# Score pieces of a fused attention and MLP kernel in other groups: three, three and two instead of four times two

## The chip, the cores and the metric

The kernel runs on one core of a Trainium2 chip. The metric is the time of the whole program on the device, in microseconds (us). Engines are named as in the profile: PE is TensorE, DVE is VectorE, ACT is ScalarE, POOL is GpSimd, SP is SyncE; PEld is the loading of weights into PE.

## What is computed

Inputs are q, k, v of 4 batches x 8 heads x 768 tokens x 64, and a matrix of 8 x 8 per batch and head, `sort_net`. In short:

```python
for _ in range(5):                       # P: rows, then columns brought to sum 1
    P = exp(P - max(P)); P /= sum(P, -1); P /= sum(P, -2)
k_sorted = P @ blocks(k)                 # 8 blocks of 96 tokens, mixed
v_sorted = P @ blocks(v)
attn = softmax(q_b @ k_sorted_b.T / 8)   # within each block of 96 tokens
x = attn @ v_sorted_b                    # -> 3072 tokens x 512
h = relu(x @ w_in)                       # 512 -> 2048
out = (s * h * h + b) @ w_out            # 2048 -> 512
```

The attention gives the 3072 x 512 input of an MLP with a hidden width of 2048. Most of the multiplications are in the MLP.

## The kernel before

**Stages.** The tokens are handled in eight tiles of 384 (a batch has two halves, `half` 0 and 1, of four blocks each). For tile `t`, `ffn1(t)` makes the hidden layer in eight steps: step `i` is 8 matmuls (L473) into a PSUM tile `hps`, then a ReLU on ACT (L485) and a square on DVE (L486). `ffn2(t)` makes the output in three rows of 128 tokens; each row is 16 matmuls (L497) into a PSUM tile `ops`, and one DVE instruction (L522) brings the row to SBUF, from which SP stores it.

**Slots.** The attention of a later tile is put between these matmuls. `ffn1` calls what its dictionary `slots` holds for step `i` after step `i`; `ffn2` has twelve slots, one after each four matmuls (slot `4*m + f//4`), the store of row `m` coming ahead of the pieces in slots 3, 7 and 11. Batch 0's second half is laid into the steps of `ffn1(0)`. Batches n = 1, 2, 3 are made by `halves(n)`, whose second dictionary `s1` fills the slots of `ffn2(2n-1)`. The order of the instructions on every engine is that of the calls; no scheduler moves them.

**Pieces.** A piece is one pair of heads (`hp`) of one half.

- `SC(b, half, hp)`, `s_piece`: 8 score matmuls (L380), two by two, each with 64 rows of K and all four blocks of both heads, into one PSUM tile `sc` of the pool `psa`; then one exponential on ACT (L388, for batch 0 L384), which writes the SBUF tile `at`.
- `SB(hp)`, `s_banks`: the same for batch 0 with the eight matmuls (L398) into two half-size PSUM tiles `scb` of the pool `psb`, and two half-size exponentials (L403).
- `P(b, half, hp)`, `p_piece`: 8 matmuls (L422) of `at` with the sorted V into a tile `pv` of `psa`; then on DVE a reciprocal (L427) and a product (L428), which writes the SBUF tile `x`.
- `V(b, i, engine)`, `v_piece`: 32 matmuls (L328) into a tile `tv` of `psa`, copied on by the engine named. `PDB(n)` is six small DVE instructions that build the mixing matrix of batch n (L273 to L282). `TD` and `TP` transpose `x`, by DMA or on PE.

The score matmuls use half of the rows of PE each, the two heads side by side; matmuls of every other large kind use all rows (the P pieces 112 of them). A run of score pieces with no other matmul between them is called a stretch here.

**Buffers.** The pool `psa` has three tiles, shared by `hps`, `sc`, `pv`, `tv` and the tiles of the sorted K; `psb` has two, shared by `ops`, `scb` and the transposes. A new tile takes the place of an old one, and its first matmul waits until the engine that reads the old one is through. PE takes its instructions in order, so all matmuls behind a waiting one wait too.

Of the kernel before, what the change touches and what calls it, by code (L numbers as in the profile page):

```python
# [22 lines left out]
def kernel(  # L23
# [182 lines left out]
    def q_banks(b, half, engs):  # L206
        if b not in QT:
            QT[b] = trp.tile([128, 2, NHP, CQ, 64], BF, tag="qt", name="qt")
        pr = slice(half * 64, (half + 1) * 64)
        for u in range(2):  # L210
            tr = psb.tile([128, 1024], BF, tag="b", name="tqb")
            for a in range(2 * u, 2 * u + 2):
                for c in range(CQ):
                    for e in range(2):
                        o = (a % 2 * CQ + c) * 64
                        nc.tensor.transpose(out=tr[e * 64:(e + 1) * 64, o:o + 64],
                                            in_=QH[b][pr, 2 * a + e, c, :],
                                            identity=ident[pr, pr])
            evac(engs[u], QT[b][:, half, 2 * u:2 * u + 2].rearrange("p a c t -> p (a c t)"),
                 tr[:, 0:2 * TG])  # L220
# [145 lines left out]
    def s_piece(b, half, hp, sc=None):  # L366
        g0 = hp * NB + half * HB
        if sc is None:
            sc = psa.tile([128, 2, 512], FP, tag="a", name="sc")
        byp = len(QT[b].shape) == 5  # L370
        for n in range(HB):
            for e in range(2):
                pr = slice(e * 64, (e + 1) * 64)
                if byp:
                    o = sc[:, e, 0:TG].rearrange("p (c t) -> p c t", c=CQ)[:, :, 16 * n:16 * n + 16]
                    r = QT[b][pr, half, hp, :, 16 * n:16 * n + 16]
                else:
                    o = sc[:, e, n * BLK:(n + 1) * BLK]
                    r = QT[b][pr, half * HB + n, hp, :]
                nc.tensor.matmul(out=o, lhsT=KS[b % 2][pr, g0 + n].rearrange("p z c -> p (z c)"),  # L380
                                 rhs=r, start=True, stop=True)
        at = atp.tile([KR, 2, TG], BF, tag="at", name="at")
        if byp:
            nc.scalar.activation(out=at.rearrange("p e (t c) -> p e t c", c=CQ),  # L384
                                 in_=sc[0:KR, :, 0:TG].rearrange("p e (c t) -> p e t c", c=CQ),
                                 func=AF.Exp, scale=scale)
        else:
            nc.scalar.activation(out=at, in_=sc[0:KR, :, 0:TG], func=AF.Exp, scale=scale)  # L388
        AT[b, half, hp] = at

    def s_banks(b, half, hp):
        g0 = hp * NB + half * HB
        at = atp.tile([KR, 2, TG], BF, tag="at", name="at")
        sc = [psb.tile([128, TG], FP, tag="b", name="scb") for _ in range(2)]
        for n in range(HB):
            for e in range(2):
                pr = slice(e * 64, (e + 1) * 64)
                nc.tensor.matmul(  # L398
                    out=sc[e].rearrange("p (c t) -> p c t", c=CQ)[:, :, 16 * n:16 * n + 16],
                    lhsT=KS[b % 2][pr, g0 + n].rearrange("p z c -> p (z c)"),  # L400
                    rhs=QT[b][pr, half, hp, :, 16 * n:16 * n + 16], start=True, stop=True)
        for e in range(2):
            nc.scalar.activation(out=at[:, e].rearrange("p (t c) -> p t c", c=CQ),  # L403
                                 in_=sc[e][0:KR].rearrange("p (c t) -> p t c", c=CQ),
                                 func=AF.Exp, scale=scale)
        AT[b, half, hp] = at

    def p_piece(b, half, hp, fill=0):
        g0 = hp * NB + half * HB
        atf = AT.pop((b, half, hp)).rearrange("p e t -> p (e t)")  # L410
        if hp == 0:
            X[b, half] = xp.tile([BLK, HB, d_model], BF, tag="x", name="x")
        x = X[b, half]
        pv = psa.tile([128, 2, 512], FP, tag="a", name="pv")
        for i in range(fill):
            nc.tensor.matmul(out=pv[:, i % 2, 272:512], lhsT=zeros[:, 0:128], rhs=zeros[:, 0:240],  # L416
                             start=True, stop=True)
        for e in range(2):
            for n in range(HB):
                c0 = (e * HB + n) * BLK  # L420
                m = 128 if c0 + 128 <= 2 * TG else BLK
                nc.tensor.matmul(out=pv[0:m, e, n * VW:(n + 1) * VW],  # L422
                                 lhsT=atf[:, c0:c0 + m], rhs=VS[b % 2][:, e * NG + g0 + n, :],
                                 start=True, stop=True)
        pvv = pv[0:BLK, :, 0:HB * VW].rearrange("p e (n w) -> p e n w", w=VW)
        rec = rtp.tile([BLK, 2, HB], FP, tag="rec", name="rec")
        nc.vector.reciprocal(out=rec, in_=pvv[:, :, :, D])  # L427
        nc.vector.tensor_tensor(  # L428
            out=x[:, :, hp * 128:(hp + 1) * 128].rearrange("p n (e d) -> p e n d", e=2),
            in0=pvv[:, :, :, 0:D],  # L430
            in1=rec.unsqueeze(3).broadcast_to([BLK, 2, HB, D]), op=ALU.mult)
# [13 lines left out]
    def t_dma(b, half):  # L445
        x = X.pop((b, half))
        xt = xtp.tile([128, HB, NHP, BLK], BF, tag="xt", name="xt")
        nc.sync.dma_start_transpose(out=xt.rearrange("p n a c -> p (n a) c"),
                                    in_=x.rearrange("p n m -> p (n m)"))
        XT[b * 2 + half] = xt  # L450
# [13 lines left out]
    def part(t, i, hpl, fill=0):  # L464
        if (t, i) not in H1:
            H1[t, i] = psa.tile([128, 2, 512], FP, tag="a", name="hps")
        for j in range(fill):
            nc.tensor.matmul(out=H1[t, i][:, j % 2, TG:512], lhsT=zeros[:, 0:128],
                             rhs=zeros[:, 0:128], start=True, stop=True)
        for f in range(2):  # L470
            for hp in hpl:
                fc = (2 * i + f) * 128
                nc.tensor.matmul(out=H1[t, i][:, f, 0:TG], lhsT=wi[:, hp, fc:fc + 128],  # L473
                                 rhs=XT[t][:, :, hp, :],
                                 start=(hp == 0), stop=(hp == NHP - 1))

    def ffn1(t, slots, done={}):

        gt = gtp.tile([128, NF, TG], BF, tag="gt", name="gt")
        GT[t] = gt  # L480
        for i in range(NF // 2):
            part(t, i, range(done.get(i, 0), NHP))
            rt = rtp.tile([128, 2, TG], BF, tag="rt", name="rt")
            h = H1.pop((t, i))[:, :, 0:TG]
            nc.scalar.activation(out=rt, in_=h, func=AF.Relu)  # L485
            nc.vector.tensor_tensor(out=gt[:, 2 * i:2 * i + 2, :], in0=rt, in1=rt, op=ALU.mult)  # L486
            for p in slots.get(i, ()):
                p()
        XT.pop(t)
# [97 lines left out]
    def QF0(): return lambda: q_banks(0, 1, "AD")  # L587
    def SB(i): return lambda: s_banks(0, 1, i)
# [3 lines left out]
    def SC(b, h, i): return lambda: s_piece(b, h, i)  # L592
    def P(b, h, i): return lambda: p_piece(b, h, i)
# [3 lines left out]
    def TD(b, h): return lambda: t_dma(b, h)  # L597
# [5 lines left out]
    def halves(n):  # L603

        if n == 1:
            s0 = {3: [KP(n, 0, "AD"), KP(n, 1, "AD"), KP(n, 2, "AD")],
                  9: [V(n, 0, "D"), V(n, 1, "A"), V(n, 2, "D")]}
        else:
            s0 = {0: [KP(n, 0), KP(n, 1), KP(n, 2)]}
        s1 = {0: [SC(n, 0, 0), SC(n, 0, 1)],  # L610
              3: [P(n, 0, 0), SC(n, 0, 2), SC(n, 0, 3)], 4: [P(n, 0, 1)], 5: [P(n, 0, 2)],
              6: [P(n, 0, 3), TD(n, 0), SC(n, 1, 0), SC(n, 1, 1)], 8: [P(n, 1, 0)],
              9: [P(n, 1, 1), SC(n, 1, 2), SC(n, 1, 3)], 10: [P(n, 1, 2)],
              11: [P(n, 1, 3), TD(n, 1)]}
        if n == 1:
            s1[0] = [V(n, 3, "A")] + s1[0]
        if n + 1 < B:
            s1[1] = [PDB(n + 1)]
        return s0, s1

    ffn1(0, {0: [QF0()], 2: [SB(0)], 3: [P(0, 1, 0), SB(1)], 4: [P(0, 1, 1), SB(2)],
             5: [P(0, 1, 2), SB(3)],
             6: [TP(0, 1, 0, "A"), TP(0, 1, 1, "D"), P(0, 1, 3)], 7: [TP(0, 1, 2, "A")]},
         {0: 3, 1: 3})
    part(1, 0, (0, 1))
# [11 lines left out]
    s0, s1 = halves(1)  # L637
    ffn2(0, s0)
    ffn2(1, s1)
    for b in range(1, B):  # L640
        n = b + 1
        s0, s1, u0, u1 = {}, {}, {}, {}
        if n < B:
            load("k", n, 6, XT[2 * b + 1][:, HB - 1, NHP - 1, 0:1])
            load_q_rows(n)
            s0, s1 = halves(n)
# [38 lines left out]
```

## Time and profile before

| What | Value |
|---|---|
| median of 3 runs | 222.98 us (222.55 to 224.73) |
| the profiled execution, whole time | 222.54 us |
| its span in the profile | 220.4 us |
| PE busy | 213.6 us, 97% |
| DVE busy | 126.0 us, 57% |
| ACT busy | 109.4 us, 50% |
| POOL busy | 70.8 us, 32% |
| score matmuls L380 / L398 | 200 and 56 |
| granted clock of PE | 0.999 |

The span leaves out what lies before the first and behind the last instruction, here 2.1 us. A row of the timeline gives the start of a run of like instructions on an engine, how long it was busy with them, the engine, the line, what is written and read, and how many they were; in brackets stands the idle time of the engine ahead of them and what ended it. Matmuls overlap, so the time that one takes of PE is read from start to start. A few matmul records are missing in the trace, so the counts of a row can be one short.

### The profile page before, as it was taken

Reading aid. Unit: us, or ns where it says so; the run is one execution under the profiler, and the core shown is the slowest. Engines: PE = TensorE matmul, PEld = TensorE weight load, DVE = VectorE, ACT = ScalarE, POOL = GpSimd, SP = SyncE. Lnnn points to the kernel's source line nnn. Section 1 sums busy time; section 2 is a strip of 40 time slices with the busy share of each in tenths; the row PEclk is TensorE's granted clock in tenths of the full one; section 3 lists DMA queues with packets and bytes.
Section 4 is the critical chain, followed back from the end, with each engine's and each line's share of the span. In section 5 each row is a group of like instructions: output and inputs, shape, how many; then the busy total and the mean of one; then the engine's idle time right before and its main releaser. Section 6 shows DMA issues by size and latency. Waiting matters only on the chain.

```text
span 220.4 us, 5172 instructions
## 1 busy us (share of the span) xinstructions
PE 213.6 (97%) x2156; PEld 128.8 (58%) x2175; DVE 126.0 (57%) x257; ACT 109.4 (50%) x149; POOL 70.8 (32%) x127
## 2 busy tenths in 40 slices
PE   7989999999999999999999999999999999999994
PEld 5877766555465555666446555665446566654454
DVE  6777457567875768547636677547417744441222
ACT  4677687658635445664622535665424356550000
POOL 7659781689832004920050008800000000000000
PEclk9999999999999999999999999999999999999999
DMA  6999999999979662999979846999911940001212
GB/s 154 284 164 125 120 170 204 204 172 134 128 215 181 49 187 41 178 208 121 141 204 175 107 135 88 208 179 102 215 72 48 123 119 3 0 0 48 93 53 95
DMA packets 67255, 28.92 MB, mean 131 GB/s; under 512 B 51872, under 2 KB 63264, under 8 KB 67232
## 3 DMA queue, kind: packets, MB, share of 16 engines
q0 software_dynamic: 31168, 12.85, 49.5%
q1 hardware_dynamic: 36064, 15.74, 35.6%
q8 instruction: 17, 0.28, 0.6%
q14 instruction: 6, 0.05, 0.1%
HBM read 28.85 MB, written 7.86 MB: 167 GB/s over the span
## 4 chain that ended last, share of the span: by engine, by line
PE 90%; DMA 5%; DVE 1%; issue 1%; POOL 1%; ACT 0%; POOLq 0%
PE hps L473 38%; PE ops L497 36%; DMA rawk<-in_k_dram 5%; PE pv L422 4%; PE sc L380 3%; PE tpp L302 2%; PE ops L514 2%; PE tv L328 2%; PE tvr L347 1%; DVE vs L204 1%; PE tr L439 1%; PE scb L398 1%; POOL rawk L93 0%; PE sc L257 0%; PE pv L416 0%
## 5 line engine op out<-in xcount | busy, mean ns | idle before, releaser
L473 PE MATMUL hps<-xt,wi 128*128 128x384 bf16 x512 | 87.9, 326 | 0.0
L497 PE MATMUL ops<-wo,gt 128*128 128x512 bf16 x350 | 82.4, 379 | 1.4 <-issue 0.6
L485 ACT ACTIVATE rt<-hps 128x768 bf16<-128x768 f32 x64 | 51.8, 811 | 39.5 <-PE hps L473 38.3
L473 PEld LDWEIGHTS <-wi 128*128 128x128 bf16 x512 | 49.0, 98 | 32.6 <-issue 0.4
L486 DVE TENSOR_TENSOR gt<-rt 128x768 bf16<-128x768 bf16 x64 | 36.0, 565 | 41.2 <-ACT rt L485 41.0
L497 PEld LDWEIGHTS <-gt 128*128 128x128 bf16 x368 | 34.1, 98 | 37.4
L522 DVE SCALAR_TENSOR_TENSOR ot<-ops,s_bc,bias 128x512 f32<-128x512 f32 (+2 forms) x27 | 18.6, 691 | 34.7 <-PE ops L497 31.6
L388 ACT ACTIVATE at<-sc 112x768 bf16<-112x768 f32 x24 | 18.1, 808 | 30.1 <-PE sc L380 30.1
L428 DVE TENSOR_TENSOR x<-pv,rec 96x512 bf16<-96x512 f32 x32 | 22.0, 686 | 1.1
L115 POOL DMA_DIRECT2D qtok<-in_q_dram x24 | 18.6, 808 | 0.7 <-issue 0.7
L422 PEld LDWEIGHTS <-at 112*128 112x128 bf16 (+1 forms) x256 | 12.9, 101 | 6.7 <-ACT at L388 1.0
L202 ACT CAST ks<-tpp 64x512 bf16<-64x512 f32 x18 | 13.2, 731 | 4.7 <-DVE ks L204 4.1
L140 POOL DMA_DIRECT2D wi<-in_moe_w_in_dram x24 | 12.8, 558 | 5.5 <-DMA rawk<-in_k_dram 3.2
L422 PE MATMUL pv<-vs,at 112*128 112x66 bf16 (+1 forms) x256 | 13.9, 195 | 0.1
L204 DVE CAST ks<-tpp 64x512 bf16<-64x512 f32 x18 | 13.1, 729 | 0.9 <-ACT ks L202 0.5
L93 POOL DMA_DIRECT2D rawk<-in_k_dram x21 | 11.2, 550 | 2.7 <-issue 1.9
L93 POOL DMA_DIRECT2D rawv<-in_v_dram x18 | 9.7, 558 | 6.0 <-DMA wo<-in_moe_w_out_dram 4.6
L130 PE MATMUL z<-zeros 128*64 128x96 bf16 (+2 forms) x129 | 9.8, 241 | 1.3 <-DVE zeros L118 1.2
L90 POOL COPY rawk<-xt 128x1 bf16<-128x1 bf16 x2 | 0.4, 190 | 32.8 <-DMA xt<-x 32.8
L427 DVE RECIPROCAL rec<-pv 96x8 f32<-96x8 f32 x32 | 6.4, 200 | 6.4 <-PE pv L422 6.4
L130 PEld LDWEIGHTS <-zeros 128*64 128x64 bf16 (+1 forms) x130 | 7.5, 115 | 3.0 <-DVE zeros L118 1.2
L349 DVE CAST rawv<-tvr 128x512 bf16<-128x512 f32 x12 | 8.2, 683 | 0.0
(93 smaller groups left out, 137.9 us busy)
## 6 DMA issues: line engine op xcount, KB each, us to landing
out_dram<-ot SPq DMA_DIRECT2D x22, 256.0 KB, 2.6
rawv<-in_v_dram POOLq DMA_DIRECT2D x18, 128.0 KB, 5.3
rawk<-in_k_dram POOLq DMA_DIRECT2D x18, 128.0 KB, 4.1
qtok<-in_q_dram POOLq DMA_DIRECT2D x24, 96.0 KB, 6.5
wo<-in_moe_w_out_dram POOLq DMA_DIRECT2D x4, 512.0 KB, 10.8
v0f<-in_v_dram SPq DMA_DIRECT2D x4, 384.0 KB, 5.9
vd<-rawv SPq DMA_DIRECT2D x4, 384.0 KB, 6.4
vs<-vd SPq DMA_DIRECT2D x8, 192.0 KB, 8.1
```

The source lines that it names most:

```text
L93: nc.gpsimd.dma_start(out=ti[:, c:c + n, :].rearrange("p c d -> p (c d)"), in_=raw["qkv".index(t)][b][:, c * D:(c + n) * D])
L115: nc.gpsimd.dma_start(out=QTOK[b][:, n], in_=qv[:, n])
L130: nc.tensor.matmul(out=z[0:m, 0:w], lhsT=zeros[:, 0:m], rhs=zeros[:, 0:w], start=True, stop=True)
L204: nc.vector.tensor_copy(out=out, in_=in_)
L388: nc.scalar.activation(out=at, in_=sc[0:KR, :, 0:TG], func=AF.Exp, scale=scale)
L422: nc.tensor.matmul(out=pv[0:m, e, n * VW:(n + 1) * VW], lhsT=atf[:, c0:c0 + m], rhs=VS[b % 2][:, e * NG + g0 + n, :], start=True, stop=True)
L428: nc.vector.tensor_tensor(out=x[:, :, hp * 128:(hp + 1) * 128].rearrange("p n (e d) -> p e n d", e=2), in0=pvv[:, :, :, 0:D], in1=rec.unsq ...
L473: nc.tensor.matmul(out=H1[t, i][:, f, 0:TG], lhsT=wi[:, hp, fc:fc + 128], rhs=XT[t][:, :, hp, :], start=(hp == 0), stop=(hp == NHP - 1))
L485: nc.scalar.activation(out=rt, in_=h, func=AF.Relu)
L486: nc.vector.tensor_tensor(out=gt[:, 2 * i:2 * i + 2, :], in0=rt, in1=rt, op=ALU.mult)
L497: nc.tensor.matmul(out=ops, lhsT=gt[:, f, m * 128:(m + 1) * 128], rhs=wo[:, f, :], start=(f == 0), stop=(f == NF - 1))
L522: nc.vector.scalar_tensor_tensor(out=ot[:, ns], in0=ops, scalar=s_bc, in1=BIAS[0][:, ns], op0=ALU.mult, op1=ALU.add)
```

## The change

In batches 1 to 3, the eight score pieces of `s1` stand in three stretches, of three, three and two pieces, at slots 0, 4 and 8, instead of four stretches of two at slots 0, 3, 6 and 9. The P pieces (0, 0), (0, 1) and (1, 0) move one slot forward, to slots 2, 3 and 7; the others stay. In batch 0's second half the four pieces, which stood alone at slots 2, 3, 4 and 5 and all went through `s_banks`, stand two by two at slots 2 and 4; the second of each two goes through `s_piece`, so it takes a tile of `psa` and one whole exponential in place of two tiles of `psb` and two half ones. No matmul is added or left out. DVE and SP have the same instructions, and ACT has two fewer: two whole exponentials stand in for four halves.

```diff
-        s1 = {0: [SC(n, 0, 0), SC(n, 0, 1)],
-              3: [P(n, 0, 0), SC(n, 0, 2), SC(n, 0, 3)], 4: [P(n, 0, 1)], 5: [P(n, 0, 2)],
-              6: [P(n, 0, 3), TD(n, 0), SC(n, 1, 0), SC(n, 1, 1)], 8: [P(n, 1, 0)],
-              9: [P(n, 1, 1), SC(n, 1, 2), SC(n, 1, 3)], 10: [P(n, 1, 2)],
-              11: [P(n, 1, 3), TD(n, 1)]}
+        s1 = {0: [SC(n, 0, 0), SC(n, 0, 1), SC(n, 0, 2)], 2: [P(n, 0, 0)], 3: [P(n, 0, 1)],
+              4: [SC(n, 0, 3), SC(n, 1, 0), SC(n, 1, 1)], 5: [P(n, 0, 2)],
+              6: [P(n, 0, 3), TD(n, 0)], 7: [P(n, 1, 0)], 8: [SC(n, 1, 2), SC(n, 1, 3)],
+              9: [P(n, 1, 1)], 10: [P(n, 1, 2)], 11: [P(n, 1, 3), TD(n, 1)]}
         if n == 1:
             s1[0] = [V(n, 3, "A")] + s1[0]
         if n + 1 < B:
             s1[1] = [PDB(n + 1)]
...
-    ffn1(0, {0: [QF0()], 2: [SB(0)], 3: [P(0, 1, 0), SB(1)], 4: [P(0, 1, 1), SB(2)],
-             5: [P(0, 1, 2), SB(3)],
+    ffn1(0, {0: [QF0()], 2: [SB(0), SC(0, 1, 1)], 3: [P(0, 1, 0)],
+             4: [P(0, 1, 1), SB(2), SC(0, 1, 3)], 5: [P(0, 1, 2)],
              6: [TP(0, 1, 0, "A"), TP(0, 1, 1, "D"), P(0, 1, 3)], 7: [TP(0, 1, 2, "A")]},
          {0: 3, 1: 3})
```

## The prediction

> **What bounds the kernel.** I read the page's busy shares first, then the chain of waits, then the waits of PE, then the timeline around the moved pieces.
>
> ```profile
> PE 213.6 (97%) x2156; PEld 128.8 (58%) x2175; DVE 126.0 (57%) x257; ACT 109.4 (50%) x149; POOL 70.8 (32%) x127
> ...
> PE 90%; DMA 5%; DVE 1%; issue 1%; POOL 1%; ACT 0%; POOLq 0%
> ```
>
> PE is busy all the time, and nine tenths of the chain is PE's; the 5% of DMA is the load of k before 14 us. In the waits of PE nothing after 20 us is longer than 0.2 us. So time is won only by taking work from PE, and every new wait of PE is lost whole: nothing later idles to give it back.
>
> **What a stretch costs PE.**
>
> ```profile
> 70.80 0.43 PE L422 MATMUL pv<-vs,at 112*128 112x66 bf16 x8
> ...
> 71.07 1.03 PE L497 MATMUL ops<-wo,gt 128*128 128x512 bf16 x4
> ...
> 71.94 0.43 PE L422 MATMUL pv<-vs,at 112*128 112x66 bf16 x8
> 72.30 0.51 PE L380 MATMUL sc<-qt,ks 64*128 64x96 bf16 x16
> ...
> 72.75 1.90 PE L497 MATMUL ops<-wo,gt 128*128 128x512 bf16 x8
> ```
>
> From start to start, a P piece takes 0.27 us before `ops` (70.80 to 71.07), but 0.36 before a stretch (71.94 to 72.30): entering costs some 0.10. The stretch of two takes 0.45 (72.30 to 72.75), that of one at 28.64 (below) 0.275; so a piece is 0.17, and leaving costs 0.45 - 0.34, some 0.10. A stretch costs 0.20 beside its pieces. One goes in each of batches 1 to 3 and two in batch 0: **-1.0 us** before waits.
>
> The Trainium skill (TensorEngine Tiling (Array Packing), Key Properties) says that a change of tiling mode drains TensorE; these rows agree, and by that rule alone the sum would end here, at 221.5. The same page (Performance Considerations, PSUM Bottleneck) says that tiling speeds up TensorE but not the emptying of PSUM, and by that the next parts decide.
>
> **Batches 1 to 3, slot 4.** The third piece there takes the `psa` tile of P(n,0,1), by the order of the instructions and their waits in the changed program; it waits for that piece's product on DVE, behind the store of row 0.
>
> ```profile
> 116.51 0.43 PE L422 MATMUL pv<-vs,at 112*128 112x66 bf16 x8
> 116.71 0.75 DVE L522 SCALAR_TENSOR_TENSOR ot<-ops,s_bc,bias 128x512 f32<-128x512 f32 x1 [2.09 <-PE ops L497]
> ...
> 117.38 0.19 DVE L427 RECIPROCAL rec<-pv 96x8 f32<-96x8 f32 x1
> 117.61 0.69 DVE L428 TENSOR_TENSOR x<-pv,rec 96x512 bf16<-96x512 f32 x1
> ```
>
> I count from the stretch's start. Three pieces end at 0.51 + 0.10 = 0.62. A slot of `ops` is 0.87 (71.07 to 71.94), so P(n,0,0) starts at 2.35 and P(n,0,1) at 3.48. The store starts 0.20 after the P piece that follows row 0 (116.71 against 116.51), at 3.69: DVE is done with P(n,0,0) by then (2.35 + 1.39, overlapping the next by 0.08). From store to the end of the product is 1.59 (116.71 to 118.30): 5.27. PE has left slot 4's `ops` at 3.48 + 0.27 + 0.87 = 4.62; after 0.10 for entering and two pieces it wants the third tile at 5.05. What PE needs after such a release is in the chain of waits:
>
> ```profile
> 16.62 0.38 ACT later L269
> 17.05 0.35 PE sc L380 x8
> ```
>
> about 0.06 from 17.00 to 17.05. So PE waits until 5.33: **0.27** in each batch. Every later release comes earlier than PE: SC(n,0,3)'s exponential ends at 5.9, P(n,0,2) starts at 6.47; slots 8 to 11 have over 1 us each. Moving PDB costs nothing: it stays in slot 1, and its DVE work (1.2 us) ends before 2.4. SP's instructions keep their order. The inputs of the pieces that move forward are there: POOL's copy that waits for batch 2's last transposed q ran at 112.17, ahead of the first stretch at 113.46, and SP issued the sorted V ahead of that; batch 3's was issued by 155.2, takes 4.5 to land, and its first stretch is at 161.99. Batches 2 and 3: -0.20 + 0.27 = **+0.07 each**.
>
> **Batch 1, slot 0.** Here V(1,3) comes first, so four tiles are asked of a pool of three: the third score piece takes the tile of V(1,3), which ACT must first copy.
>
> ```profile
> 64.31 0.69 PE L328 MATMUL tv<-pd,vp 128*64 128x64 bf16 x32
> ...
> 64.94 0.52 PE L380 MATMUL sc<-qt,ks 64*128 64x96 bf16 x16
> 65.05 1.02 ACT L202 CAST vs<-tv 112x1024 bf16<-112x1024 f32 x1 [2.81 <-PE tv L328]
> ```
>
> PE wants it at 64.94 + 0.34 = 65.28; the copy ends at 66.07, and with 0.06 PE goes on at 66.13: 0.85. ACT was idle before the copy, so it can't start earlier. Batch 1: -0.20 + 0.85 + 0.27 = **+0.92**.
>
> **Batch 0.** Here `hps` tiles share `psa` with the new `sc`.
>
> ```profile
> 28.64 0.34 PE L398 MATMUL scb<-qt,ks 64*128 64x96 bf16 x8
> 28.74 0.81 ACT L485 ACTIVATE rt<-hps 128x768 bf16<-128x768 f32 x1 [0.39 <-PE hps L473]
> ...
> 28.91 1.47 PE L473 MATMUL hps<-xt,wi 128*128 128x384 bf16 x8
> 29.45 0.87 ACT L403 ACTIVATE at<-scb 112x384 bf16<-112x384 f32 x2
> ```
>
> A step of `hps` takes 1.31 of PE. On the clock of this trace:
>
> - Stretch at 28.64, `hps` 3 at 29.09, P(0,1,0) at 30.40, `hps` 4 due at 30.67. It takes the tile of SC(0,1,1), whose exponential stands on ACT behind the ReLU of step 2 and two halves (29.45 + 0.87 = 30.32) and ends at 31.02 (0.81, overlapping by 0.1). `hps` 4 starts at 31.08: **0.41**.
> - The ReLU of step 3 follows that exponential and ends at 31.73. In the trace the ReLU of 30.42 to 31.23 is followed by square, reciprocal and product, the product ending at 32.66, 1.43 later: now 33.16. P(0,1,1) runs at 32.39, the stretch from 32.76; SC(0,1,3), due at 32.93, takes P(0,1,0)'s tile and starts at 33.22: **0.28**.
> - `hps` 5 starts at 33.49, P(0,1,2) is due at 34.80; its tile is that of SC(0,1,3), whose exponential ends at 34.87: **0.12**.
> - `hps` 6 goes from 35.19 to 36.50; transposes and P(0,1,3) take 0.61; `hps` 7, due at 37.11, takes P(0,1,2)'s tile. The ReLU of step 5 ends at 35.81, so that product at 37.24; start at 37.30: **0.19**.
>
> Before, `hps` 7 started at 36.74: 0.56 later now, of which 0.02 comes back from a wait of the trace at 38.87. The drains saved are in this figure. Batch 0: **+0.54**.
>
> **Sum.** 0.54 + 0.92 + 0.07 + 0.07 = +1.6 us. The profiled execution took 222.54 (span 220.4 and 2.1 around it): 224.1. The median of the runs lies 0.44 above that execution, so I say **224.4**, halfway. Bounds: the drains are measured; a wait in a stretch isn't in this trace except the 0.06 after ACT, so each of the eight waits can be shorter, down to nothing if the tile comes free some other way, or longer, by up to a further leaving and entering of 0.20 for each of the five that stand inside a stretch. I take 0.06, the only row of the kind.
>
> **Rivals.**
>
> - *Only the drains count* (the tiles don't bind): 222.54 - 1.0 = 221.5. For it: PE waited for nothing before. Against: the changed program has these waits, and ACT's copy takes 1.02 us in the trace. 3%.
> - *Only the copy of V binds*; DVE and ACT run a little ahead of my walk, whose other waits are mostly under 0.3: -1.0 + 0.85 = 222.4, not slower than before. For it: 0.3 is a small difference of long sums. Against: the walk puts together only durations that repeat here within 0.02. 10%.
> - *Slower*: a wait inside a stretch costs a drain and a refill more, 5 x 0.20 = 1.0: 225.1, or 225.4 from where I start. It decides from 0.12 per wait, where the sum passes 1%. Against it: after 17.00 the score matmuls started with no such loss. 14%.
> - Forecast: 73%.
>
> **Chances and range.** About 1% (2.2 us) is what a measurement can tell from no change. The forecast and both rivals below it lie within 1%; the slower rival lies beyond, and so does some of the forecast's own upper edge, 3%. Faster by over 1%: 2%, for what I haven't seen, since no case here gives it; within: 81%; slower: 17%. The forecast alone goes from 223.5 to 225.1 (the waits 0.3 shorter and the runs' 0.44 left out, or as much longer); with most of the slower rival, and the upper part of the second, the range is 223.0 to 225.6.
>
> **What would show it.** In the profile after: three score stretches of 24, 24 and 16 matmuls per batch; PE idle ahead of L380 with ACT `vs` as its releaser, some 0.8 us, once; about 0.3 us before L380 three times with DVE `x`; and PE waits at L473 in 30 to 38 us with ACT `at` and DVE `x`. `hps` 7 of tile 0 starts near 37.3. It is wrong if those waits aren't there, or if PE waits at slots 8 to 11.

## The result and the profile after

The changed kernel is slower by 0.64%: the median is 224.25 us (224.0 to 225.09, 17 runs) against 222.78 us before (222.47 to 224.73, 17 runs), a ratio of 1.0064 with a 95% interval of 1.0053 to 1.0076. (Here and below the ratio and its interval come from all fast runs and not from the two medians, so they can differ a little from the medians' quotient.) The profiled execution took 224.12 us with a span of 222.0, 1.6 more than before's 222.54 and 220.4.

The page of the changed kernel, busy time of each engine and the chain of waits by engine:

```profile
PE 213.7 (96%) x2156; PEld 128.5 (58%) x2175; DVE 125.8 (57%) x257; ACT 108.7 (49%) x147; POOL 71.0 (32%) x127
...
PE 92%; DVE 5%; issue 1%; ACT 1%
```

PE is about as long busy as before (213.7 us against 213.6) in a span that is 1.6 longer, and it has the same matmuls, so the difference is idle time of PE. The row is no finer than some 0.6 us: a second profile of the same changed kernel (e7) has 213.1. DVE has gone from 1% of the chain to 5%, ACT from nothing to 1%. Such a share is not the loss: 5% of 222.0 us is 11 us, while all waits read below come to 2.7 us. (The 5% of DMA that the chain of before held at its start is gone from this one, since here the chain goes back through other work before 14 us.)

**Where the time came in.** One execution starts its main part up to 0.8 us later than another, with the same program up to there, so I compare stage by stage, from start to start on PE:

| Stage on PE | before | after | change | forecast |
|---|---|---|---|---|
| batch 0: from the q transposes (L216) at 26.03 to the bias matmuls (L576) | 18.99 | 19.50 | +0.51 | +0.54 |
| batch 1's slots: from V(1,3) (L328 at 64.31) to the next ffn1 | 14.40 | 15.30 | +0.91 | +0.92 |
| batch 2's slots: from the first score matmul (L380 at 113.46) to the next ffn1 | 13.77 | 13.84 | +0.07 | +0.07 |
| batch 3's slots: the same at 161.99 | 13.77 | 13.84 | +0.07 | +0.07 |

The four add up to 1.55 us before rounding, and the span is 1.6 us longer, so the rest of the program takes the same time.

**Batch 1, slot 0**, timeline of the changed kernel (start, busy time, engine, line, what is written and read, number of instructions, idle time before and its releaser):

```profile
64.82 0.70 PE L328 MATMUL tv<-pd,vp 128*64 128x64 bf16 x32
...
65.45 0.51 PE L380 MATMUL sc<-qt,ks 64*128 64x96 bf16 x16
65.56 1.02 ACT L202 CAST vs<-tv 112x1024 bf16<-112x1024 f32 x1 [2.81 <-PE tv L328]
...
66.63 0.35 PE L380 MATMUL sc<-qt,ks 64*128 64x96 bf16 x8 [0.66 <-ACT vs L202]
```

The third piece was due at 65.45 + 0.34 = 65.79 and starts at 66.63, 0.05 after the copy's end at 66.58: a wait of 0.84. The row says 0.66, since the idle time is counted from the modelled end of the matmuls ahead; from start to start is what PE lost.

**Batch 2, slot 4**, the same view:

```profile
118.36 0.43 PE L422 MATMUL pv<-vs,at 112*128 112x66 bf16 x8
118.57 0.75 DVE L522 SCALAR_TENSOR_TENSOR ot<-ops,s_bc,bias 128x512 f32<-128x512 f32 x1
...
119.23 0.19 DVE L427 RECIPROCAL rec<-pv 96x8 f32<-96x8 f32 x1
119.46 0.69 DVE L428 TENSOR_TENSOR x<-pv,rec 96x512 bf16<-96x512 f32 x1
...
119.59 0.96 PE L380 MATMUL sc<-qt,ks 64*128 64x96 bf16 x24
...
120.20 0.20 PEld L380 LDWEIGHTS <-ks 64*128 64x128 bf16 x8 [0.24 <-DVE x L428]
```

The stretch of 24 takes 0.96 here, and 0.68 in slot 0 of the same batch (114.88): 0.28 more. The eight weight loads of its third piece wait for DVE's product (119.46 + 0.69 = 120.15) and start at 120.20. The product stands behind the store of 118.57.

**Batch 0**, the same view:

```profile
30.19 0.82 ACT L384 ACTIVATE at<-sc 112x768 bf16<-112x768 f32 x1
...
30.39 0.43 PE L422 MATMUL pv<-vs,at 112*128 112x66 bf16 x8
...
31.06 1.46 PE L473 MATMUL hps<-xt,wi 128*128 128x384 bf16 x8 [0.24 <-ACT at L384]
...
33.19 0.20 PEld L380 LDWEIGHTS <-ks 64*128 64x128 bf16 x8 [0.27 <-DVE x L428]
...
34.01 0.82 ACT L384 ACTIVATE at<-sc 112x768 bf16<-112x768 f32 x1
...
34.88 0.43 PE L422 MATMUL pv<-vs,at 112*128 112x66 bf16 x8
...
36.53 0.69 DVE L428 TENSOR_TENSOR x<-pv,rec 96x512 bf16<-96x512 f32 x1
...
37.27 0.77 PEld L473 LDWEIGHTS <-wi 128*128 128x128 bf16 x6 [0.16 <-DVE x L428]
```

Step 4 of `ffn1(0)`, due 0.27 after 30.39, starts at 31.06, when the whole exponential of SC(0,1,1) is through (30.19 + 0.82 = 31.01). SC(0,1,3) at 33.19 waits for DVE's product; P(0,1,2) starts at 34.88, behind the whole exponential of SC(0,1,3) (34.01 + 0.82 = 34.83); step 7 starts at 37.28, behind the product that ends at 36.53 + 0.69 = 37.22. All four waits of the forecast are there: from start to start 0.40, 0.29, 0.10 and 0.22 us.

### The profile page after: what moved, and what is told of

Its sections match the earlier page's. It is cut to its first block, busy times and chain, and to the rows that moved or that the text cites. A ratio compares the mean times of both kernels' runs of the same rounds, so it can differ in the third digit from the quotient of the medians.

```text
span 222.0 us, 5167 instructions
## 1 busy us (share of the span) xinstructions
PE 213.7 (96%) x2156; PEld 128.5 (58%) x2175; DVE 125.8 (57%) x257; ACT 108.7 (49%) x147; POOL 71.0 (32%) x127
## 4 chain that ended last, share of the span: by engine, by line
PE 92%; DVE 5%; issue 1%; ACT 1%
PE hps L473 37%; PE ops L497 34%; PE z L130 5%; PE pv L422 3%; PE sc L380 2%; PE tpp L302 2%; PE tv L328 2%; PE ops L514 2%; DVE x L428 1%; DVE ot L522 1%; PE tvr L347 1%; DVE vs L204 1%; PE tr L439 1%; PE tp L292 1%; PE sc L257 0%
## 5 line engine op out<-in xcount | busy, mean ns | idle before, releaser
L380 PE MATMUL sc<-qt,ks 64*128 64x96 bf16 x216 | 7.4, 204 | 1.3 <-ACT vs L202 0.7
```

## The experiments

The theory is that a stretch costs PE some 0.2 us beside its pieces, so that the regrouping saves 1.0 us, and that waits for tiles of the pool `psa` cost more than that at three places: four waits in batch 0, the copy of V(1,3) in batch 1, and the product behind the store at slot 4 of batches 1 to 3. The rivals are that one part of the regrouping alone is to blame, that the drains around a stretch are worth nothing, and that a stretch of three is dear in itself.

### Each part alone

`e1_batch0_only` has the new slots of batch 0 and the old `s1`; `e2_later_only` the reverse.

```diff
 e1, against the kernel before
-    ffn1(0, {0: [QF0()], 2: [SB(0)], 3: [P(0, 1, 0), SB(1)], 4: [P(0, 1, 1), SB(2)],
-             5: [P(0, 1, 2), SB(3)],
+    ffn1(0, {0: [QF0()], 2: [SB(0), SC(0, 1, 1)], 3: [P(0, 1, 0)],
+             4: [P(0, 1, 1), SB(2), SC(0, 1, 3)], 5: [P(0, 1, 2)],
```

> The kernel before with batch 0's stretches alone regrouped (two of two pieces), batches 1 to 3 as before. Theory of the psa tiles: two stretches fewer save 0.4 us, four waits of PE in steps 3 to 7 of the first ffn1 cost 0.9; in sum +0.5 us, a ratio of 1.0023 to before, and hps 7 of tile 0 starts near 37.3 us instead of 36.7. Rival, the regrouping of batches 1 to 3 alone makes the kernel slower, since a stretch of three costs more than its pieces: -0.4 us, a ratio of 0.998.

> The changed kernel with batch 0 as before, so batches 1 to 3 alone in stretches of three, three and two. Theory of the psa tiles: batch 1 +0.9 us, batches 2 and 3 +0.07 each, in sum +1.0 us, a ratio of 1.0047. Rival, batch 0 alone makes the kernel slower and the tiles of the later batches come free in time: -0.6 us, a ratio of 0.997.

| Kernel | median, us | ratio to before | 95% interval | batch 0's stage | from the bias matmuls to the end |
|---|---|---|---|---|---|
| before | 222.83 | | | 18.99 | 175.40 |
| e1_batch0_only | 223.15 | 1.0009 | 0.9996 to 1.0023 | 19.51 | 175.39 |
| e2_later_only | 223.79 | 1.0038 | 1.0025 to 1.0051 | 18.99 | 176.46 |

In the traces each part carries its own loss and leaves the other stage as it was: +0.52 and +1.06 us, which add up to 1.58 where both together lost 1.55. The times agree for the later batches. For batch 0 alone they are weak: the interval takes in no change as well as the forecast 1.0023, which lies at its very edge, and leaves out only the rival's 0.998. That the loss of batch 0 is real rests on the trace, on the same 0.51 to 0.52 us in every profile with this part (19.50 to 19.51 us in five of them), and on `e8` below.

### More stretches and no wait

`e3_more_stretches` takes apart two stretches per batch of the kernel before.

```diff
-        s1 = {0: [SC(n, 0, 0), SC(n, 0, 1)],
+        s1 = {0: [SC(n, 0, 0)], 2: [SC(n, 0, 1)],
...
-              6: [P(n, 0, 3), TD(n, 0), SC(n, 1, 0), SC(n, 1, 1)], 8: [P(n, 1, 0)],
+              6: [P(n, 0, 3), TD(n, 0), SC(n, 1, 0)], 7: [SC(n, 1, 1)], 8: [P(n, 1, 0)],
```

> The kernel before with the stretches at slots 0 and 6 of batches 1 to 3 taken apart, their second pieces one or two slots later (slots 2 and 7): six stretches more, and by my walk through the slots no new wait of PE. If a stretch costs 0.20 us beside its pieces: +1.2 us, a ratio of 1.0054. If the gaps around a stretch lie beside other work and only waits count: no change, 1.000.

Measured: 224.25 us against 222.83, a ratio of 1.0057 (1.0038 to 1.0076). From the bias matmuls to the end it is 176.66 us, 1.26 more than before, or 0.21 for each of the six stretches, with the same matmuls and no new wait of PE in the trace. Its timeline on PE, batch 2:

```profile
121.16 0.43 PE L422 MATMUL pv<-vs,at 112*128 112x66 bf16 x8
121.52 0.34 PE L380 MATMUL sc<-qt,ks 64*128 64x96 bf16 x8
121.80 1.04 PE L497 MATMUL ops<-wo,gt 128*128 128x512 bf16 x4
122.77 0.34 PE L380 MATMUL sc<-qt,ks 64*128 64x96 bf16 x8
123.04 1.04 PE L497 MATMUL ops<-wo,gt 128*128 128x512 bf16 x4
```

Four `ops` that stand between two stretches take 0.97 (121.80 to 122.77) instead of 0.87, and a lone piece 0.275. So the saving that the change was credited with is real: it is given back, not absent.

### The two waits of the later batches, one at a time

`e4_v_early` and `e5_p_pair` are the changed kernel with one edit each; `e7_after_again` is the changed kernel beside them on the same chip.

```diff
 e4, against the changed kernel
-                  9: [V(n, 0, "D"), V(n, 1, "A"), V(n, 2, "D")]}
+                  9: [V(n, 0, "D"), V(n, 1, "A"), V(n, 2, "D")], 10: [V(n, 3, "A")]}
...
-        if n == 1:
-            s1[0] = [V(n, 3, "A")] + s1[0]

 e5, against the changed kernel
-        s1 = {0: [SC(n, 0, 0), SC(n, 0, 1), SC(n, 0, 2)], 2: [P(n, 0, 0)], 3: [P(n, 0, 1)],
+        s1 = {0: [SC(n, 0, 0), SC(n, 0, 1), SC(n, 0, 2)], 2: [P(n, 0, 0), P(n, 0, 1)],
```

> The changed kernel with one edit: V(1,3) at slot 10 of the ffn2 ahead, so that ACT has copied its tile before the stretch of three at slot 0 of batch 1 asks for it. Theory: the wait of 0.85 us of the third score piece goes and the rest stays, +0.7 us against before, a ratio of 1.0032. Rival, PE waits there for the exponentials or for something else behind them: as the changed kernel, 1.0065.

> The changed kernel with one edit: P(n,0,1) at slot 2 behind P(n,0,0), so that its DVE work stands ahead of the store of row 0 and not behind it. Theory: the wait of 0.27 us of the third piece at slot 4 goes in each of three batches, 0.8 us less than the changed kernel, +0.7 us against before, a ratio of 1.0032. Rival, the store isn't the cause (the third piece waits for PE's own leaving and entering, or for ACT): as the changed kernel, 1.0065.

> The changed kernel itself, beside the two edits of it on the same chip: +1.5 us, a ratio of 1.0065.

| Kernel | median, us | ratio to before (222.93) | 95% interval | from the bias matmuls to the end |
|---|---|---|---|---|
| e7_after_again | 224.25 | 1.0053 | 1.0027 to 1.0079 | 176.44 |
| e4_v_early | 223.47 | 1.0042 | 1.0011 to 1.0072 | 175.72 |
| e5_p_pair | 223.52 | 1.0015 | 0.9990 to 1.0041 | 175.60 |

These intervals are wide and overlap. That of e5 takes in the theory's 1.0032 and leaves out the rival's 1.0065; that of e4 takes in both (three of its 12 runs took 225 us), so for e4 the times alone decide nothing. The medians of e4 and e5 lie 0.8 and 0.7 us below e7's, and the stage is shorter by 0.72 and 0.84 in the traces, where 0.85 and 0.81 were expected. In e4, timeline on PE, batch 1:

```profile
63.76 1.90 PE L497 MATMUL ops<-wo,gt 128*128 128x512 bf16 x8
65.60 0.69 PE L380 MATMUL sc<-qt,ks 64*128 64x96 bf16 x24
```

ACT copies V(1,3) from 63.87 to 64.89, ahead of the stretch at 65.60, and the stretch of 24 has no wait. In e5, timeline of batch 2:

```profile
117.50 1.89 PE L497 MATMUL ops<-wo,gt 128*128 128x512 bf16 x8
...
118.51 0.69 DVE L428 TENSOR_TENSOR x<-pv,rec 96x512 bf16<-96x512 f32 x1
119.11 0.74 DVE L522 SCALAR_TENSOR_TENSOR ot<-ops,s_bc,bias 128x512 f32<-128x512 f32 x1
...
119.32 0.68 PE L380 MATMUL sc<-qt,ks 64*128 64x96 bf16 x24
```

With the product ahead of the store, the stretch of 24 has no wait: 0.68 instead of 0.96. The edit brings the piece a slot earlier as well, so by itself it doesn't tell the store from the time. The rows do: a product with nothing ahead of it on DVE ends 1.40 us after its P piece starts (118.19 to 118.90 + 0.69 in the kernel before), so by this estimate it would have ended at 118.36 + 1.40 = 119.76 in the changed kernel, and PE wants the tile only at 119.59 + 0.34 = 119.93. So the store was the cause at slot 4, and the tile of V at slot 0. That e4 gave 0.12 us less in the trace than the wait it removed fits the place of V(1,3): it now stands between `ops`, where it goes in and out by itself, while before it stood next to the scores and shared one change with them (the last section has the numbers).

### Batch 0: the grouping or the tiles

`e8_batch0_tiles` regroups nothing, but takes the second and fourth piece through a tile of `psa`, as the change does.

```diff
-    ffn1(0, {0: [QF0()], 2: [SB(0)], 3: [P(0, 1, 0), SB(1)], 4: [P(0, 1, 1), SB(2)],
-             5: [P(0, 1, 2), SB(3)],
+    ffn1(0, {0: [QF0()], 2: [SB(0)], 3: [P(0, 1, 0), SC(0, 1, 1)], 4: [P(0, 1, 1), SB(2)],
+             5: [P(0, 1, 2), SC(0, 1, 3)],
```

> The kernel before with nothing regrouped: batch 0's pieces stand alone at slots 2, 3, 4 and 5 as before, but the second and the fourth go through a psa tile and one whole exponential, as they do in the changed kernel. Theory of the psa tiles: the two extra tiles in the pool make PE wait 0.4 us at hps 4 (for the ReLU of step 3), 0.2 at the fourth piece (for DVE's product) and 0.2 at hps 6 (for the ReLU of step 5); +0.8 us, a ratio of 1.0035, and the stage from the transposes of q to the bias matmuls grows by 0.8 us. So batch 0's regrouping would itself be worth 0.3 to 0.4 and the tiles more than that. Rival, two pieces in one stretch pile their exponentials up ahead of a ReLU and that alone is the loss: no change, 1.000.

Measured: 223.69 us against 222.92, a ratio of 1.0034 (1.0022 to 1.0045); batch 0's stage takes 19.75 us, 0.76 more than before, and the rest as before (175.41). Its timeline on PE:

```profile
31.44 0.34 PE L380 MATMUL sc<-qt,ks 64*128 64x96 bf16 x8
32.08 1.46 PE L473 MATMUL hps<-xt,wi 128*128 128x384 bf16 x8 [0.30 <-ACT rt L485]
...
35.87 0.34 PE L380 MATMUL sc<-qt,ks 64*128 64x96 bf16 x8
36.39 1.46 PE L473 MATMUL hps<-xt,wi 128*128 128x384 bf16 x8 [0.17 <-ACT rt L485]
```

Steps 4 and 6 start 0.64 and 0.52 after the lone pieces, which take 0.275 in `e3`: waits of 0.37 and 0.24 for ReLUs. (The lone piece at 35.87 waits 0.18 for DVE.) Two more tiles in a pool of three are enough for the loss, without any regrouping, and the regrouped batch 0 (+0.51) is 0.25 us better than that; 0.3 to 0.4 was expected. So the grouping in batch 0 isn't what costs; the tiles that it needs are.

### The later batches without their waits

`e6_no_waits` puts the edits of e4 and e5 together and leaves batch 0 as it was before; `e9_no_waits_again` is the same kernel on another occasion.

> The changed kernel with its waits taken away: batch 0 as before, V(1,3) at slot 10 of the ffn2 ahead instead of just before the stretch of three, and P(n,0,1) at slot 2 behind P(n,0,0), so that its product stands on DVE ahead of the store of row 0. Batches 1 to 3 keep their stretches of three, three and two. Theory of the psa tiles: three stretches fewer and no wait, -0.6 us, a ratio of 0.9973, faster than before. Rival, a stretch of three costs more than its pieces or collides with the P pieces that moved forward: still slower than before, a ratio of 1.002 or more.

> The kernel with the changed grouping of batches 1 to 3 and its waits taken away, again, on this chip: -0.6 us, less 0.1 for V(1,3), which now stands alone between output matmuls, a ratio of 0.9975. Rival: no change.

Measured: 222.12 us against 222.83, a ratio of 0.9973 (0.9957 to 0.9989), and 222.43 against 222.92, a ratio of 0.9969 (0.9955 to 0.9983). It is faster than both kernels, by 0.3% than the kernel before. From the bias matmuls to the end it takes 174.86 and 174.87 us in the two profiles, 0.5 less than before: three stretches of 0.2, less some 0.1 for V(1,3). (The profiled execution of e6 has a wait of its own in batch 0, 0.34 us for the load of q; e9's batch 0 takes 18.99 as before.) Timeline of e9 on PE, batch 1:

```profile
62.92 0.69 PE L328 MATMUL tv<-pd,vp 128*64 128x64 bf16 x32
63.55 1.90 PE L497 MATMUL ops<-wo,gt 128*128 128x512 bf16 x8
65.38 0.69 PE L380 MATMUL sc<-qt,ks 64*128 64x96 bf16 x24
66.23 1.67 PE L497 MATMUL ops<-wo,gt 128*128 128x512 bf16 x7 [0.16 <-issue]
...
70.10 0.68 PE L380 MATMUL sc<-qt,ks 64*128 64x96 bf16 x24
```

The two stretches of 24 take 0.69 and 0.68, with no releaser beside them. (The 0.16 at 66.23 stands at a matmul record that is missing.) The same groups of three, three and two that lose 1.0 us in the changed kernel win 0.5 here, so a stretch of three isn't dear in itself.

## Why the prediction was right, point by point

- **PE bounds the kernel, and each new wait is lost whole**: right. What the four stages lost, 1.55 us, is in the span at the end, 1.6 us longer; nothing later gave it back.
- **A stretch costs 0.20 beside its pieces; five fewer save 1.0**: right; six more cost 1.26 in e3, 0.21 each. The Trainium skill, TensorEngine Tiling (Array Packing), says in Key Properties that a change of tiling mode drains TensorE; the trace agrees, with some 0.1 us lost at each change into and out of the scores. PSUM Bottleneck on the same page says that tiling doesn't speed up the emptying of PSUM; the trace agrees here too, with 2.7 us of waits for tiles of `psa` against 1.0 us saved.
- **Slot 4, 0.27 in each batch**: right (0.27), and by the mechanism named: with the product ahead of the store in e5, the wait was gone.
- **Slot 0 of batch 1, 0.85**: right (0.84); e4 took it away.
- **Batch 0, four waits of 0.41, 0.28, 0.12 and 0.19, +0.54**: measured 0.40, 0.29, 0.10 and 0.22, and +0.51. The waits sum to 1.01 us; two stretches fewer take off 0.4, and two small waits of the kernel before are gone: some 0.06 in the P piece at 30.22, which waited for the second half exponential (29.45 + 0.87 = 30.32), and 0.02 at 38.87. The price of a release, 0.06, was 0.05 or 0.06 in these rows.
- **The sum, +1.6 us**: 1.55 in the trace; by the medians 224.25 - 222.78 = 1.47.
- **The time, 224.4**: 0.15 high. The sum on the profiled execution alone, 224.1, was nearer to the 224.12 of the profiled execution after. The half of 0.44 that I put on top was too much: over 17 runs the median of before lies 0.24 above its profiled execution.
- **The rivals**: the drains alone (221.5) and V's copy alone (222.4) fell with the trace, which has all the waits. The slower one, a further drain for a wait inside a stretch, fell too: after the waits at 66.63 and 120.20 the third piece goes on as any other.

What I had not priced is that V(1,3) pays for going in and out as well, and shares one change with the scores beside it. It had no part in this change, but it took some 0.1 us of the remedy.

## What to carry to other kernels

Where matmuls that use half of the rows stand among full ones, read the price of a group from start to start on PE, and put groups together; but count the tiles that the larger group holds at once, and for each tile the next owner takes, walk through the engine that frees it, with everything that is queued ahead of it there. Here more tiles asked of a pool of three cost 2.7 us of waits where the grouping saved 1.0. In the later batches the waits stood at a copy of 1.0 us and behind a store of 0.75 us, and moving two pieces ahead of these turned a loss of 1.0 us there into a gain of 0.5 without touching the groups.

## What was unexpected on the hardware

The 32 matmuls of a V piece (128 rows, 64 columns) pay as well when they stand among full ones. In the trace of e4 an `ops` starts 0.216 us after the `ops` before it, but V(1,3) starts 0.309 after its last one: 0.09 for going in. V's own matmuls come in twos 0.03 apart, but the next `ops` starts 0.129 after the last of them: 0.10 for coming out. To the scores, in the kernel before, it is 0.128, so V next to a stretch pays for one change there, and not for two.

In the kernel before, `ops` to V(1,3) to the scores thus needed one change less than in e4, where both stand alone, and e4 gave 0.72 us in the trace where the wait that it removed was 0.84. The difference, 0.12 us, is about the 0.1 of one change. No run moves V(1,3) and nothing else about the waits, so this fits the starts but wasn't tried by itself.

The 48 transposes of q (L216, 64 rows and 64 columns) show the same price in the kernel before: the first starts 0.253 us after the last `hps`, where `hps` follow each other at 0.162. The P pieces, with 112 rows, show none: 0.27 us for eight of them among `ops`, one after the other at 0.03, the first 0.216 after an `ops` and the next `ops` 0.041 after the last.
